# Value loads of batches 3 to 7 spread over their own batch, and q/k loads of batches 4 to 7 moved five steps later, in a fused attention and feed-forward kernel

## The chip, the cores and the metric

One core of one Trainium2 chip. The metric is the device time of one execution in microseconds (us); lower is better. TensorE is called PE, its weight loads PEld, VectorE DVE, ScalarE ACT, GpSimd POOL and SyncE SP; "SPq" is SP's sequencer, which here only issues transfers. Each run lists its mean granted TensorE clock; 1.000 is full speed. A kernel's runs are compared with runs of the kernel before on the same chip.

## The reference

Sliding-window attention with a linear position bias, 8 batches, 8 heads, 576 positions, 64 values a head, then a feed-forward layer on the 4608 rows of 512:

```python
scores = scale * np.matmul(q, k.transpose(0, 1, 3, 2))
mask = (rel >= 0) & (rel < 128)
scores = np.where(mask, scores + bias[None], -1000000000.0)
attn = np.exp(scores - np.max(scores, axis=-1, keepdims=True))
attn = attn / (np.sum(attn, axis=-1, keepdims=True) + 1e-09)
x = (attn @ v).transpose(0, 2, 1, 3).reshape(4608, 512)
h = x @ w_in                                   # 512 -> 2048
out = (h * (1.0 / (1.0 + np.exp(-beta * h)))) @ w_out
```

## The kernel before

A batch has five blocks of rows (128, 128, 128, 128, 64). From batch 3 on, each block of q and k takes this way: SP loads it in float32 (256 KB each), POOL casts it to bfloat16, SP transposes it by DMA into `QK[b % 2]`. Values are loaded and cast in one transfer that POOL issues. The order of all instructions on PE, SP and POOL is fixed by hand: `merge` puts "jobs" at places counted in steps of PE's attention work, and the feed-forward matmuls of earlier batches are spread between the steps.

```python
def load_v(b, sb):
    to = VS[b % 2][0 : ROWS[sb], sb, :, 0:D]
    if b >= NTE:                                    # NTE = 3
        nc.gpsimd.dma_start(out=to, in_=v[b, :, ...].rearrange("h p d -> p h d"))
        return
    ...
def TD(b, sb):                                      # q, then k
    for i in range(2):
        nc.sync.dma_start_transpose(out=QK[b % 2][:, i, :, P * sb : ...], in_=...)
...
for b in range(NTE, B):
    for sb in range(NQB):
        casts = []
        t0 = first[b] - 26 + 4.3 * sb               # first[b]: step of the first scores
        jobs.append((t0, lambda ...: c.append(load_qk(b, sb))))
        jobs.append((t0 + 4.5, lambda c=casts: c.pop()()))
        jobs.append((t0 + 8.5, lambda ...: TD(b, sb)))
        vals(b, sb, first[b] - 7 + 3 * sb)
...
jobs.sort(key=lambda j: j[0])
```

The scores of a batch come in four visits of PE (`SC`, matmuls `sps`). The first two need q of blocks 0 to 2 and k of blocks 0 and 1; the third is the first to need block 4. In the feed-forward part `hps` is the first matmul and `ops` the second.

The softmax here doesn't subtract the row's maximum and nothing guards it: scores larger than these inputs give would overflow.

## Time and profile before

| | |
|---|---|
| time | 332.25 us, median of 3 runs (331.75 to 333.48) |
| PE busy | 318.6 of 329.8 us |
| longest wait of PE | 2.5 us, once, at 95.6 us, for a transpose of batch 3 |
| mean clock of the profiled run | 0.995 |

The prediction below shows the lines of PE, of the wait and of SP's queue. What POOL did meanwhile is in its timeline (start, length, engine, what, idle before):

```profile
81.20 0.89 POOL L137 DMA_DIRECT2D vs<-in_v_dram  x1
...
85.61 0.61 POOL L129 CAST bst<-fst 64x512 bf16<-64x512 f32 x1 [1.37 <-DMA fst<-in_k_dram]
86.17 0.88 POOL L137 DMA_DIRECT2D vs<-in_v_dram  x1
87.04 0.57 POOL L413 DMA_DIRECT2D out_dram<-osb  x1
87.61 0.89 POOL L137 DMA_DIRECT2D vs<-in_v_dram  x1
```

The cast at 85.61 is that of batch 3's last block; its transposes were issued only at 90.24 and after. Between them lie loads of batch 4 on SP, and loads of batch 3's values on POOL.

### The profile page before, as it was taken

How to read it: one execution, taken by the hardware profiler on the slowest of the kernel's cores; microseconds unless marked ns; L12 is line 12 of the kernel's file. 1: busy time of each engine (PE TensorE's matmuls, PEld its weight loads, DVE VectorE, ACT ScalarE, POOL GpSimd, SP SyncE). 2: the span in 40 equal slices, each digit the busy share in tenths (PEclk: the TensorE clock that was granted, in tenths of full speed). 3: DMA queues.
4: the chain of work that ended last, by engine and by line, in shares of the span. 5: the costliest groups of instructions: out<-in, count | busy, mean ns of one | idle time of the engine just before them, and what ended most of it. 6: DMA issues, size and time to landing. Idle time of an engine off the chain costs nothing.

```text
span 329.8 us, 6229 instructions
## 1 busy us (share of the span) xinstructions
PE 318.6 (97%) x2300; PEld 155.8 (47%) x2300; DVE 193.2 (59%) x421; ACT 213.4 (65%) x414; POOL 107.4 (33%) x173
## 2 busy tenths in 40 slices
PE   8999999999969999999999999999999999999995
PEld 3454455445534555454445444544455444444442
DVE  6678679983435776666666766666665543344310
ACT  5657776878756777777777777777774444454421
POOL 4756492244542652614334423530000000000000
PEclk9999999999998999999999999999999999999999
DMA  7999999999999999799999999893121210001111
GB/s 198 252 205 279 192 262 211 220 179 176 167 225 219 197 205 214 108 156 164 185 178 128 152 143 231 122 167 51 40 66 55 79 35 32 34 32 56 41 66 64
DMA packets 136174, 47.67 MB, mean 145 GB/s; under 512 B 123200, under 2 KB 133712, under 8 KB 136144
## 3 DMA queue, kind: packets, MB, share of 16 engines
q1 hardware_dynamic: 105744, 31.60, 51.8%
q0 software_dynamic: 30224, 15.54, 32.8%
q8 instruction: 18, 0.29, 0.4%
q10 hardware_dynamic: 176, 0.14, 0.1%
q14 instruction: 12, 0.10, 0.1%
HBM read 36.71 MB, written 9.44 MB: 140 GB/s over the span
## 4 chain that ended last, share of the span: by engine, by line
PE 85%; DMA 5%; DVE 4%; SPq 3%; ACT 1%; issue 1%; POOL 1%; POOLq 0%
PE hps L379 36%; PE ops L395 33%; PE sps L290 5%; DMA fst<-in_k_dram 4%; PE pv L334 3%; PE pv L330 2%; SPq L253 2%; PE sps L276 2%; PE w L218 1%; PE tps L229 1%; DMA qkT<-bst 1%; DVE qkT L234 1%; DVE gT L385 1%; PE xt L359 1%; SPq L95 1%
## 5 line engine op out<-in xcount | busy, mean ns | idle before, releaser
L384 ACT ACTIVATE sig<-hps,beta_h 128x512 bf16<-128x512 f32 x144 | 99.8, 695 | 78.7 <-PE hps L379 64.0
L379 PE MATMUL hps<-XT,W 128*128 128x512 bf16 x576 | 147.4, 379 | 0.5 <-DVE gT L385 0.4
L395 PE MATMUL ops<-W,gT 128*128 128x512 bf16 x576 | 146.3, 381 | 0.1
L385 DVE SCALAR_TENSOR_TENSOR gT<-sig,hps 128x512 bf16<-128x512 bf16 x144 | 98.3, 684 | 64.2 <-ACT sig L384 63.7
L395 PEld LDWEIGHTS <-gT 128*128 128x128 bf16 x576 | 53.6, 98 | 63.1 <-issue 2.9
L379 PEld LDWEIGHTS <-W 128*128 128x128 bf16 x576 | 51.7, 98 | 52.9 <-issue 3.5
L303 ACT ACTIVATE pt<-sps,bias 128x256 bf16<-128x256 f32 (+1 forms) x192 | 72.9, 493 | 4.1 <-PE sps L290 4.1
L129 POOL CAST bst<-fst 128x512 bf16<-128x512 f32 (+1 forms) x50 | 32.9, 659 | 77.7 <-DMA fst<-in_q_dram 51.2
L307 DVE TENSOR_TENSOR pt<-pt,mask 128x1024 bf16<-128x1024 bf16 x48 | 34.4, 718 | 37.3 <-ACT pt L303 37.1
L413 POOL DMA_DIRECT2D out_dram<-osb x32 | 17.9, 560 | 94.1 <-ACT osb L410 94.1
L340 DVE TENSOR_TENSOR xn<-pv,zs 128x256 bf16<-128x256 f32 (+1 forms) x80 | 33.7, 423 | 2.6
L410 ACT ACTIVATE osb<-ops 128x512 f32<-128x512 f32 x35 | 20.9, 597 | 15.2 <-PE ops L395 15.2
L334 PE MATMUL pv<-vs,pt 128*128 128x65 bf16 x320 | 28.6, 193 | 0.3 <-DVE qkT L234 0.3
L334 PEld LDWEIGHTS <-pt 128*128 128x128 bf16 x320 | 21.6, 97 | 10.3 <-issue 0.6
L290 PE MATMUL sps<-qkT 64*128 64x256 bf16 (+2 forms) x320 | 22.2, 254 | 3.4 <-DMA qkT<-bst 2.5
L330 PE MATMUL pv<-vs,pt 128*128 128x65 bf16 x256 | 24.0, 193 | 0.3 <-DVE XT L365 0.3
L330 PEld LDWEIGHTS <-pt 128*128 128x128 bf16 x256 | 20.1, 98 | 7.3 <-issue 0.7
L290 PEld LDWEIGHTS <-qkT 64*128 64x128 bf16 x320 | 11.4, 95 | 22.1 <-issue 14.8
L298 ACT ACTIVATE pt<-sps 128x1024 bf16<-128x1024 f32 x16 | 16.3, 1023 | 8.2 <-PE sps L290 7.7
L137 POOL DMA_DIRECT2D vs<-in_v_dram x25 | 21.4, 855 | 0.3 <-issue 0.2
L339 DVE RECIPROCAL zs<-pv 128x4 f32<-128x4 f32 (+1 forms) x80 | 13.9, 175 | 9.6 <-PE pv L334 9.4
L113 POOL CAST bst<-fst 128x512 bf16<-128x512 f32 x24 | 14.4, 617 | 13.8 <-DMA fst<-in_q_dram 11.3
(49 smaller groups left out, 113.3 us busy)
## 6 DMA issues: line engine op xcount, KB each, us to landing
fst<-in_q_dram SPq DMA_DIRECT2D x32, 256.0 KB, 4.7
fst<-in_k_dram SPq DMA_DIRECT2D x32, 256.0 KB, 5.1
out_dram<-osb POOLq DMA_DIRECT2D x32, 256.0 KB, 3.5
fst<-in_v_dram SPq DMA_DIRECT2D x12, 256.0 KB, 6.5
vs<-in_v_dram POOLq DMA_DIRECT2D x20, 128.0 KB, 5.1
W<-in_moe_w_in_dram POOLq DMA_DIRECT2D x4, 512.0 KB, 7.2
W<-in_moe_w_out_dram POOLq DMA_DIRECT2D x4, 512.0 KB, 13.7
fst<-in_q_dram SPq DMA_DIRECT2D x8, 128.0 KB, 4.1
```

The source lines that it names most:

```text
L129: nc.gpsimd.tensor_copy(out=t[0 : ROWS[sb], i], in_=f)
L137: nc.gpsimd.dma_start(out=to, in_=v[b, :, P * sb : P * sb + ROWS[sb], :].rearrange("h p d -> p h d"))
L290: nc.tensor.matmul(o, lhsT=qk[64 * e : 64 * e + 64, 1, p, P * kb : P * kb + P], rhs=qk[64 * e : 64 * e + 64, 0, p, P * kb : P * kb + nq], ...
L303: nc.scalar.activation(out=pt[:, e, cols], in_=sps[e][:, cols], func=ACTF.Exp, scale=qscale, bias=bias[:, half, h : h + 1],)
L307: nc.vector.tensor_tensor(out=pt[:], in0=pt[:], in1=masks[m][:].rearrange("p (o c) -> p o c", o=1).broadcast_to([P, 2, 512]), op=ALU.mult,)
L330: nc.tensor.matmul(pv[:, hl, 0 : D + 1], lhsT=weights(b, qb - 1, h, 1), rhs=vs[:, qb - 1, h, 0 : D + 1], start=True, stop=False,)
L334: nc.tensor.matmul(pv[:, hl, 0 : D + 1], lhsT=weights(b, qb, h, 0), rhs=vs[:, qb, h, 0 : D + 1], start=qb == 0, stop=True,)
L340: nc.vector.tensor_tensor(out=xn[0:nq, 4 * g : 4 * g + 4, :], in0=pv[0:nq, :, 0:D], in1=zs[0:nq].broadcast_to([nq, 4, D]), op=ALU.mult,)
L379: nc.tensor.matmul(hps[:], lhsT=W1[:, c, bass.ts(j, P)], rhs=XT[:, c, c0 : c0 + TOKG], start=(c == 0), stop=(c == NDM - 1),)
L384: nc.scalar.activation(out=sig[:], in_=hps[:], func=ACTF.Tanh, scale=beta_h[:, j : j + 1])
L385: nc.vector.scalar_tensor_tensor(out=gts[g][:, j, :], in0=sig[:], scalar=1.0, in1=hps[:], op0=ALU.add, op1=ALU.mult)
L395: nc.tensor.matmul(ops_[:], lhsT=gT[:, j, i * P : i * P + P], rhs=W2[:, j, :], start=(j == 0), stop=(j == NFF - 1),)
```

## The change

The intent: take other transfers out of the way of batch 3's last transposes, and make the rest pay for it as late as they can. In steps, batch 4's first two loads stood at first[3] - 5 and first[3] - 0.7, batch 3's last transposes at first[3] - 0.3; after the change the loads stand at first[3] and later.

```diff
-                t0 = first[b] - 26 + 4.3 * sb
+                t0 = first[b] - (26 if b == NTE else 21) + 4.3 * sb
...
-                vals(b, sb, first[b] - 7 + 3 * sb)
+                vals(b, sb, first[b] + 4.3 * sb - 0.5)
```

## The prediction

> **What bounds the kernel now.** I read the page first (busy shares and slices), then who PE waited for, then the chain of waits around the one long wait, then short windows for the clock, and last the timelines of the two queues that issue transfers. The page says that TensorE is the bound, with one visible dent:
>
> ```profile
> PE 318.6 (97%) x2300; PEld 155.8 (47%) x2300; DVE 193.2 (59%) x421; ACT 213.4 (65%) x414; POOL 107.4 (33%) x173
> ...
> PE   8999999999969999999999999999999999999995
> ...
> PEclk9999999999998999999999999999999999999999
> DMA  7999999999999999799999999893121210001111
> ```
>
> Each slice is 8.2 us. From the second slice on PE is full except in slice 12 (counted from 1), around 91 to 99 us, and the clock digit dips right behind it. DMA digits are at 9 until about 215 us and near 1 after it, so the loads are front-loaded. The longest wait of PE, by who ended it (total, times, longest):
>
> ```profile
> PE sps L290 <- DMA qkT<-bst: 2.5, 1, 2.5
> ```
>
> One wait, once, 2.5 us: a score matmul of batch 3 waits for a DMA transpose of q and k. The next is 1.2 us at the very start, the rest 0.8 us and less. The chain of waits (start, length, what) shows it and what follows:
>
> ```profile
> 93.88 4.19 DMA qkT<-bst
> 98.07 0.05 issue
> 98.12 0.82 PE sps L290 x10
> 98.94 1.82 PE ops L395 x4
> 100.76 1.07 PE hps L379 x4
> ```
>
> and the same kind of visit undisturbed, 34 us later:
>
> ```profile
> 132.77 0.55 PE sps L290 x12
> 133.31 0.97 PE ops L395 x4
> 134.28 0.86 PE hps L379 x4
> ```
>
> The transpose landed at 98.07. The four ops matmuls behind the wait took 1.82 instead of 0.97 us. The windows (PE, PEld, DVE, ACT, POOL busy; then clock, DMA share, GB/s) say why:
>
> ```profile
> 97.00:98.00 1.00, 0.00 (x0) 0.00 (x0) 0.00 (x0) 0.00 (x0) 0.93 (x2) 0.81 1.03 205
> 98.00:99.00 1.00, 0.88 (x11) 0.63 (x12) 0.00 (x0) 0.45 (x2) 0.00 (x0) 0.50 1.41 163
> ```
>
> The granted clock was half from about 97.6 to 101.04 (0.81 is 0.38 us at half, then three windows at 0.50, then 0.98, which is 0.04 us: 3.4 us). Finally the queue that issues q/k loads and transposes (SP, in order):
>
> ```profile
> 80.40 0.66 SPq L95 DMA_DIRECT2D fst<-in_q_dram  x1
> 81.11 0.62 SPq L95 DMA_DIRECT2D fst<-in_k_dram  x1
> 81.78 0.62 SPq L95 DMA_DIRECT2D fst<-in_q_dram  x1
> 82.44 0.61 SPq L95 DMA_DIRECT2D fst<-in_k_dram  x1
> 83.16 5.13 SPq L253 DMA_TRANSPOSE qkT<-bst  x2
> ...
> 90.24 7.50 SPq L253 DMA_TRANSPOSE qkT<-bst  x4
> ```
>
> The loads at 80.40 and 81.11 are batch 3's last rows; 81.78 and 82.44 are already batch 4's. The pair at 83.16 transposes batch 3's fourth block, and the first two of the four at 90.24 its fifth, the one PE waits for. The pair before, at 77.56, took 2.78 us to issue; here it took 5.1, and the first transpose at 90.24 held the queue until about 93.8. Its cast was done at 86.22 (GpSimd timeline: 85.61 plus 0.61), so data was not the reason, the queue was. In the same stretch GpSimd issued value loads of batch 3 at 81.20, 86.17, 87.61 and 90.63, and the DMA share rose to 2.43 in 86:88 and 2.96 in 88:90 (1.26 at 78:80, with 260 GB/s) while 88:90 moved 65 GB/s.
>
> **What the Trainium skill says.** "DMA: Bandwidth & Descriptors", section Anatomy of one DMA: a semaphore wait happens on the issuing sequencer before dispatch, so what stands ahead in SP's queue delays what follows. The order above agrees. Same page, section Issuing engines are not separate DMA queues: transfers started by any engine end on the same 16 DMA engines and interleave. The trace fits (transposes slow where GpSimd's value loads are in flight), though it does not prove it. "TensorE: Matmul & The Clock Gate", section Part 1: The HAM clock gate: after an idle window of about 3.4 us the clock drops to 4/8, and windows are free-running, 3413 ns. The 3.4 us at 0.50 agree; here an idle of only 2.5 us was enough. These waits therefore cost twice: the idle, and the half-speed stretch behind it.
>
> **The change part by part.** No arithmetic is touched. The order of PE, DVE and ACT instructions is the same in both builds except for buffer numbers; SP and GpSimd are reordered.
>
> 1. Batch 4's q/k loads move five steps later, so in SP's order batch 3's fourth and fifth transposes now stand before any load of batch 4. A step: batches 4 and 5 start their scores at 115.93 and 149.18 in PE's timeline, 33.25 us for 23 steps, 1.45 us each; five are 7.2 us. Estimate for the fifth block: its k load was issued at 81.11; with fewer transfers beside it, it lands by about 84.5, the cast ends by 85.1, two transposes (1.2 to 2 us each) are issued by 88, landing by 91. PE wants it just after 95.33, so some 4 us to spare. The wait goes.
>
> 2. Batch 3's value loads no longer come ahead of its first scores (five at first score minus 7 and every 3 steps before; now minus 0.5 and every 4.3). This takes three or four 128 KB loads out of 81 to 92 us. Values are first used long after: at 102.53, 111.43, 113.64, 120.18, 129.53 for the five blocks. In GpSimd's new order they follow the stores and would be issued near 86, 88, 95, 98 and 108; at 5 us to landing each is early by 5 us or more. No new wait of PE on values.
>
> 3. What comes off the path. In the undisturbed visit, ops starts 0.55 us after the first score matmul; so without the wait it would start at 95.33 + 0.55 = 95.88, instead of 98.94: 3.06 us. The half clock then costs (1.82 - 0.97) + (1.07 - 0.86) = 1.06 us. Together 4.1 us. Behind it PE is without gaps to the end (20.00 of 20 us in every 20 us window from 100 to 300), so every microsecond gained there arrives at the end, unless a new gap takes it.
>
> 4. The price: later transposes for batches 4 to 7. Landing of the third block's q transposes against the first score, before: batch 4 110.0 against 115.93, batch 5 133.2 against 149.18, batch 6 170.9 against 181.69, batch 7 207.8 against 214.32. Moved 7.2 us, batches 4 and 7 would be late by 1.3 and 0.7 us if all else kept its time. But it doesn't: batch 4's chain suffered from the same congestion, and batch 7's stood behind X transposes.
>
> **The rivals.** (a) *The wait is gone and nothing replaces it*: 332.25 - 4.1 = 328.1. For: the slack in 1 and 2. (b) *The wait moves to batch 4's first scores*. In the new order, estimated from loads at about 88, casts 1.5 us, pairs of 2.8 us and about 5 us per block, its third block lands near 109 to 110; PE would be there at 115.93 - 4.1 = 111.8. Two microseconds of slack, and a miss costs 1 to 2 us, plus up to 1 us of clock: 329 to 331. (c) *X transposes hold the queue*. In the new order the third block of batches 5, 6 and 7 stands just behind an X transpose that needs the attention output of the batch before (ready at 141.1, 173.7 and 206.2, in times of before). The scores follow 8.0 us later each time. Before, from an X issue to the landing of the next q transpose took 3.6 to 7.2 us. So it mostly fits, but each is a place for a stall of up to 1.5 us: 329 to 331. (d) *The gain is hidden by another engine*. Against: ACT 65% and DVE 59%, and no other wait of PE over 0.5 us after 60 us. (e) *Congestion and not order was the cause, and the value loads only carry it elsewhere*: then new stalls spread over batches 4 to 7, near 332. Against: from 130 us on pairs issue in about 2.5 us with the old value loads beside them.
>
> **Range and chances.** I take 4.1 us off, and give back 0.4 us for (b) and (c) (about one chance in three of a stall of some 1.3 us): 328.5 us. The runs of before spread from 331.75 to 333.48, so the range is 327.2 to 331.0. Faster by over 2% would need under 325.6, more than PE's idle time and cold stretch after start-up hold: 0.02. Slower by over 2%: 0.01. Within 2%: 0.97.
>
> **What would show it.** Right: no wait of PE for the transposes at batch 3, no clock below 1.00 between 90 and 110 us, the SP queue issuing batch 3's last pair before 88, PE busy up from 97% to 98%, and ops at the same place starting about 3 us earlier with 0.97. Wrong: a new wait of PE on these transposes just before the first scores of batch 4, 5, 6 or 7 (near 112, 145, 178, 210 us), a wait of PE on values, or a second half-clock stretch.

## The result, and the profile after

329.75 us, median of 6 runs (328.62 to 330.53), against 333.51 us for the kernel before in 6 runs (331.75 to 335.15). The ratio is 0.9889, 95% interval 0.9851 to 0.9928, an interval that leaves out 1; two runs of the kernel before against itself, below, show how far such an interval can be trusted. (A ratio is the mean time of one kernel's runs over that of the other's runs of the same rounds, so not quite the ratio of the medians. Executions over 1.5% slower than the fastest of the same kernel are left out of the means.) The page of the profile after:

```profile
PE 315.0 (96%) x2258; PEld 155.4 (47%) x2300; DVE 194.4 (59%) x421; ACT 213.6 (65%) x414; POOL 106.8 (33%) x173
...
PE   8889999999999999999999999999999999999995
...
PEclk9999999999999999999999999999999999999999
DMA  7999999999799999989999999999222200001011
```

The 6 in PE's digits and the 8 in the clock's are gone. PE's busy time fell as well, from 318.6 to 315.0 us, though that is not all gain: 42 of its 2300 matmul records are missing here, and a cold matmul counts as longer busy. The prediction's sign "PE busy up from 97% to 98%" did not come: it is 96% here, and 97% in a second profile with all records. DMA is at 9 up to the same place, or one slice later, so nothing was saved there, only moved. PE's waits between 80 and 240 us in the profile after (total, times, longest) begin with:

```profile
PE sps L290 <- DMA qkT<-bst: 0.2, 1, 0.2
```

2.5 us have become 0.2, and the 0.2 is elsewhere: at 113.9 us, the first scores of batch 4. The queue of SP after, at the same place as before:

```profile
81.49 0.66 SPq L95 DMA_DIRECT2D fst<-in_q_dram  x1
82.20 0.62 SPq L95 DMA_DIRECT2D fst<-in_k_dram  x1
82.94 6.04 SPq L253 DMA_TRANSPOSE qkT<-bst  x4
89.03 0.59 SPq L95 DMA_DIRECT2D fst<-in_q_dram  x1
89.67 0.89 SPq L95 DMA_DIRECT2D fst<-in_k_dram  x1
```

All four transposes of batch 3's last two blocks go out right behind their own loads, the last by 88.98, and batch 4's loads follow. And PE at the visit where it had waited:

```profile
96.98 0.61 PE L290 MATMUL sps<-qkT 64*128 64x256 bf16 x12
97.53 1.04 PE L395 MATMUL ops<-W,gT 128*128 128x512 bf16 x4
98.40 1.03 PE L379 MATMUL hps<-XT,W 128*128 128x512 bf16 x4
```

Twelve score matmuls in one go, and `ops` four in 0.87 us from start to next start (1.68 before, 98.87 to 100.55).

Times in the two traces can't be laid side by side, since this run reached batch 3 1.65 us later (its start-up has waits of 1.1 us for weights that the first profile lacks). So measure from batch 3's first score to batch 4's first: 32.20 us before (83.72 to 115.93), 28.25 after (85.37 to 113.62). The difference, 3.95 us, is what the change did in these two profiles. It is more than the spans' difference of 2.0 us, mostly because of the later start.

### The profile page after: what moved, and what is told of

Same layout as the page of the kernel before. It is cut to its first block, busy times and chain, and to the rows that moved or that the text cites. A ratio compares the mean times of both kernels' runs of the same rounds, so it can differ in the third digit from the quotient of the medians.

```text
span 327.8 us, 6185 instructions
## 1 busy us (share of the span) xinstructions
PE 315.0 (96%) x2258; PEld 155.4 (47%) x2300; DVE 194.4 (59%) x421; ACT 213.6 (65%) x414; POOL 106.8 (33%) x173
## 4 chain that ended last, share of the span: by engine, by line
PE 59%; DMA 22%; SPq 8%; POOL 4%; ACT 3%; DVE 2%; issue 2%; POOLq 0%
PE ops L395 29%; PE hps L379 25%; DMA fst<-in_k_dram 11%; DMA fst<-in_v_dram 6%; SPq L253 4%; DMA fst<-in_q_dram 3%; PE sps L290 2%; DMA qkT<-bst 2%; SPq L109 2%; SPq L95 2%; ACT pt L303 2%; PE pv L334 2%; POOL bst L129 1%; PE pv L330 1%; DVE gT L385 1%
## 5 line engine op out<-in xcount | busy, mean ns | idle before, releaser
L379 PE MATMUL hps<-XT,W 128*128 128x512 bf16 x554 | 144.0, 379 | 2.1 <-DMA W<-in_moe_w_in_dram 1.1
L395 PE MATMUL ops<-W,gT 128*128 128x512 bf16 x560 | 143.7, 379 | 1.4 <-issue 0.3
L129 POOL CAST bst<-fst 128x512 bf16<-128x512 f32 (+1 forms) x50 | 31.9, 645 | 78.2 <-DMA fst<-in_q_dram 52.8
L307 DVE TENSOR_TENSOR pt<-pt,mask 128x1024 bf16<-128x1024 bf16 x48 | 35.3, 735 | 34.6 <-ACT pt L303 34.4
L113 POOL CAST bst<-fst 128x512 bf16<-128x512 f32 x24 | 14.3, 619 | 13.5 <-DMA fst<-in_q_dram 8.8
## 6 DMA issues: line engine op xcount, KB each, us to landing
W<-in_moe_w_out_dram POOLq DMA_DIRECT2D x4, 512.0 KB, 13.4
```

The source lines that it names most:

```text
L129: nc.gpsimd.tensor_copy(out=t[0 : ROWS[sb], i], in_=f)
L307: nc.vector.tensor_tensor(out=pt[:], in0=pt[:], in1=masks[m][:].rearrange("p (o c) -> p o c", o=1).broadcast_to([P, 2, 512]), op=ALU.mult,)
L379: nc.tensor.matmul(hps[:], lhsT=W1[:, c, bass.ts(j, P)], rhs=XT[:, c, c0 : c0 + TOKG], start=(c == 0), stop=(c == NDM - 1),)
L395: nc.tensor.matmul(ops_[:], lhsT=gT[:, j, i * P : i * P + P], rhs=W2[:, j, :], start=(j == 0), stop=(j == NFF - 1),)
```

## The experiments

Theory A, mine after the prediction: either part alone is enough, since each takes a delay out. Theory B: the order in SP's queue alone decides. Theory C: the value loads' congestion alone decides. The second question was the size: how much of the gain is the wait, how much the half clock behind it, and is it there in every run? In order of time, the first four runs (values alone, q/k alone, PE kept busy, kernel before again) and the last four (changed kernel again, batch 4 rematch, kernel before a third time, four earlier) were on one chip (called A), the four between on another (B). On each chip the runs of the kernel before, to which ratios refer, are shared.

### The value loads alone

```diff
-                vals(b, sb, first[b] - 7 + 3 * sb)
+                vals(b, sb, first[b] + 4.3 * sb - 0.5)
```

> The value loads spaced as in the changed kernel, q and k of batches 4 to 7 as before, so two loads of batch 4 still stand ahead of batch 3's last transposes. Theory A (either part alone is enough, each takes one of two delays out): no wait of PE at batch 3 over 0.5 us, the pair of transposes for the fifth block issued by 89 us, time ratio to before 0.987 to 0.993. Theory B (only the order in the SP queue counts): a wait of 1.5 us or more stays and a half-clock stretch follows, ratio 0.997 to 1.003. Theory C (only the congestion by value loads counts): as A here.

Measured: 330.85 us, ratio 0.9916 (0.9868 to 0.9963). PE's wait between 80 and 240 us, then SP's queue:

```profile
PE sps L290 <- DMA qkT<-bst: 1.8, 1, 1.8
```

```profile
83.52 0.63 SPq L95 DMA_DIRECT2D fst<-in_q_dram  x1
84.19 0.78 SPq L95 DMA_DIRECT2D fst<-in_k_dram  x1
85.08 5.18 SPq L253 DMA_TRANSPOSE qkT<-bst  x2
90.31 0.59 SPq L95 DMA_DIRECT2D fst<-in_q_dram  x1
90.95 0.57 SPq L95 DMA_DIRECT2D fst<-in_k_dram  x1
91.63 7.26 SPq L253 DMA_TRANSPOSE qkT<-bst  x4
```

No value load is left before or beside the pair of transposes at 85.08, and it still takes 5.18 us to issue (5.13 before). Two of the four value loads are left by the next pair (89.20 and 91.91), and the four transposes take 7.26 us (7.50 before). The wait stays, so theory A falls for batch 3; theory C falls with the next run, which has no wait with all the old value loads in place. Theory B is right about the wait, but its half clock and its ratio (0.997 to 1.003) did not come. The time alone would have misled: the ratio lies in the range of theory A. Why it does comes below, with the clock.

### The q and k loads alone

```diff
-                t0 = first[b] - 26 + 4.3 * sb
+                t0 = first[b] - (26 if b == NTE else 21) + 4.3 * sb
```

> The q and k loads of batches 4 to 7 five steps later, value loads as before, so batch 3's value loads still run into its last transposes. Theory A: no wait of PE at batch 3 over 0.5 us, ratio 0.987 to 0.993; the first transposes of the fourth and fifth block may take 2 to 3 us to issue, but they start about 5 us earlier. Theory B (order): as A. Theory C (congestion by value loads): a wait of 1.5 us or more stays, ratio 0.997 to 1.003.

Measured: 331.17 us, ratio 0.9938 (0.9890 to 0.9986). No wait at batch 3, as B says, but the page is not clean:

```profile
PE sps L290 <- DMA qkT<-bst: 4.9, 3, 2.2
```

Three new waits: 1.86 us at batch 4's first scores, 0.84 at batch 6's, 2.18 at batch 7's. None of my theories had them here. Before batch 7, POOL and SP of this run:

```profile
206.33 1.79 POOL L137 DMA_DIRECT2D vs<-in_v_dram  x2
208.11 0.58 POOL L413 DMA_DIRECT2D out_dram<-osb  x1
```

```profile
208.02 1.21 SPq L355 DMA_TRANSPOSE XT<-xn  x1
209.34 3.61 SPq L253 DMA_TRANSPOSE qkT<-bst  x2
```

and of the changed kernel:

```profile
205.61 0.70 POOL L137 DMA_DIRECT2D vs<-in_v_dram  x1
206.30 0.58 POOL L413 DMA_DIRECT2D out_dram<-osb  x1
```

```profile
206.06 2.06 SPq L355 DMA_TRANSPOSE XT<-xn  x1
208.24 2.51 SPq L253 DMA_TRANSPOSE qkT<-bst  x2
```

With two value loads and a store just ahead, the third block's q transpose took 6.5 us from issue to landing, that is, to the arrival of its data (209.34 to 215.87); with one and a store, 3.6 us (208.24 to 211.84). Five steps later, the third block's transpose falls among the old, bunched value loads, and it has no time to spare. So the two parts aren't two cures for one wait: the later q/k loads cure batch 3, and the spread values pay for the later q/k loads. The 4.9 us are those of this run's slowest execution, the profiled one (333.24 us); by the medians of chip A, bunched values cost some 1.6 us (331.17 against 329.57 of the changed kernel again).

### How much each pair of loads in front costs

Two runs vary the number of batch 4's load pairs ahead of batch 3's last transposes: one (values spread as in the change), and three plus a pair of transposes (values as before).

```diff
# three_later, against the changed kernel
-                t0 = first[b] - (26 if b == NTE else 21) + 4.3 * sb
+                t0 = first[b] - (26 if b == NTE else 23) + 4.3 * sb
# four_earlier, against the kernel before
-                t0 = first[b] - 26 + 4.3 * sb
+                t0 = first[b] - (30 if b == NTE + 1 else 26) + 4.3 * sb
```

> The changed kernel with q and k of batches 4 to 7 three steps later instead of five: one pair of loads of batch 4 stands ahead of batch 3's last pair of transposes, none ahead of the pair before it. If each pair of loads in front costs its own delay (theory of the order): the last transpose lands 1 to 5 us before PE wants it, no wait of PE at batch 3 over 0.5 us, and batches 4 to 7 have 1 to 3 us more to spare than in the changed kernel, so no wait at all there; ratio 0.985 to 0.992. If any load in front is enough to lose: a wait of 1 us or more at batch 3, ratio 0.992 to 0.999.

> The kernel before with batch 4's q and k four steps earlier still: three pairs of loads and one pair of transposes of batch 4 then stand ahead of batch 3's last pair of transposes instead of two pairs of loads. Measured from batch 3's first score, that transpose landed at about 4.3 us with no pair in front, 8.6 with one, 13.4 with two; at some 4.5 us for each pair it lands at 18 to 22 now, and PE wants it at 11.9: a wait of 6 to 10 us, with a half clock of 3.4 us or more in it and behind it. Ratio 1.010 to 1.025. If the wait has nothing to do with what stands in front, it stays at 1.5 to 3 us and the ratio at 1.00.

Measured: one pair 329.54 us, ratio 0.9950 (0.9913 to 0.9986, chip B); three pairs 338.67 us, ratio 1.0155 (1.0085 to 1.0225, chip A). SP's queue with one pair in front (the loads at 85.47 and 86.10):

```profile
82.82 2.59 SPq L253 DMA_TRANSPOSE qkT<-bst  x2
85.47 0.58 SPq L95 DMA_DIRECT2D fst<-in_q_dram  x1
86.10 0.56 SPq L95 DMA_DIRECT2D fst<-in_k_dram  x1
86.78 4.17 SPq L253 DMA_TRANSPOSE qkT<-bst  x2
```

The pair with no load of batch 4 in front goes out in 2.59 us, the one behind two loads in 4.17. Landing of batch 3's last transpose, from batch 3's first score, by the trace; PE wants it at 11.9:

| pairs of loads in front | landed at, us | wait of PE, us |
|---|---|---|
| none (changed kernel, twice) | 6.9, 7.5 | none |
| none, value loads as before (q/k alone) | 7.9 | none |
| one | 9.0 | none |
| two, values spread | 13.6 | 1.8 |
| two (kernel before, three profiles) | 14.3, 13.8, 15.1 | 2.5, 1.9, 3.2 |
| three and a pair of transposes | 17.8 | 5.7 |

Four more profiles with none in front, all with spread values (the two of batch 4 alone, eight later, batch 7's values bunched), gave 6.7 to 8.3 us. So the loads in front decide, with about 1 to 6 us for each pair; the old value loads can't be seen with none in front (7.9), and with two in front the kernel before is 0.1 to 1.4 us later than the run with spread values. The table gives k's transpose, the last; the expectation for three pairs counted from q's, which landed at 4.3 (none), 8.6 (one), 13.4 (two) and here 17.4 us (three). No run issued the same loads at the same time from another queue, so whether it is their place in SP's queue or their traffic that delays the transposes is not told apart; moving them later removes both. The wait with three pairs, 5.7 us, came out just under the 6 to 10 I expected. The one-pair version met its expectation at batch 3, but not at the end, where it had a wait of 0.5 us at batch 7, nor in its ratio (0.985 to 0.992 expected).

### PE kept busy during the wait

```diff
-            SC(b, m, p)
+            SC(b, m, p, fill=12 if (b, m, p) == (NTE, 1, 0) else 0)
```

> The kernel before, with 12 matmuls of zeros (512 columns each, 12 x 0.216 = 2.6 us) ahead of batch 3's first score matmul of its second half, into the same PSUM bank that it then starts afresh: PE stays busy while the transpose lands. The result stays right. If the half clock behind the wait comes from the idle, no record shows a clock under 1.00 near 98 to 101 us, the ops matmuls behind take 0.97 us instead of 1.82, and the time falls by about 1.0 us (ratio 0.995 to 0.999, if the transpose lands when it did). If the clock drops for another reason (load, chance), it stays at half for 3.4 us there and the time is the same or longer.

Measured: 332.38 us, ratio 0.9962 (0.9919 to 1.0005), result correct. PE of this run:

```profile
96.54 2.75 PE L218 MATMUL sps<-zero 128*128 128x512 bf16 x12
99.23 0.61 PE L290 MATMUL sps<-qkT 64*128 64x256 bf16 x12
99.78 1.04 PE L395 MATMUL ops<-W,gT 128*128 128x512 bf16 x4
```

No idle, no half clock, `ops` at full speed. As expected; but a single profile without a half clock proves little, as the next run shows. More telling: none of the six executions had a mean clock of 0.995 or less, against 13 of 24 of the kernel before on this chip (below). And from batch 3's first score to batch 4's it took 30.75 us against 32.20 in the first profile, with the transpose landing nearly as late (14.0 and 14.3 us after the first score). That puts the half clock's own cost at 1.2 to 1.4 us. The interval of the time includes 1, so by time it is open; the median isn't below the 331.41 us of the kernel before's runs at clock 1.000, so no gain beyond the clock is to be seen.

### The kernel before, again

> The kernel before itself, for a second profile: the wait at batch 3 again, 1.5 to 4 us, followed by a half-clock stretch of 3.4 us or a multiple; ratio 0.997 to 1.003. It shows how far the start (the first 60 us) moves from profile to profile: if the changed kernel's later start of about 1.7 us is chance, this one's start differs from the first profile's by something like it.

> The kernel before, a third profile: a wait of 1.5 to 3 us at batch 3. If the rule is that the clock halves when PE idles about 2 us or more inside one window of a fixed 3.41 us grid, this profile shows a half-clock stretch only if one of its windows holds 2.0 us of the idle, and none if the grid splits it below 1.9. Ratio 0.996 to 1.004, which also shows what this comparison can resolve.

Measured: 331.82 us, ratio 0.9954 (0.9893 to 1.0014); and 331.21 us, ratio 0.9937 (0.9890 to 0.9985). The second interval leaves out 1 for the very same code, and both ratios lie outside what I had expected of it (0.997 to 1.003 and 0.996 to 1.004): the comparison resolves no better than some 0.6%, and the half-clock stretch expected of the first did not come. Windows of the second profile (us, busy times, then clock, DMA share, GB/s), and then of the third:

```profile
97.00:98.00 1.00, 0.00 (x0) 0.00 (x0) 0.52 (x1) 0.45 (x1) 1.00 (x2) 1.00 0.98 275
98.00:99.00 1.00, 0.14 (x6) 0.14 (x8) 0.17 (x1) 0.00 (x0) 0.75 (x2) 1.00 0.78 133
99.00:100.00 1.00, 1.00 (x14) 0.53 (x9) 0.00 (x0) 0.81 (x3) 0.00 (x0) 1.00 1.26 115
```

```profile
98.00:99.00 1.00, 0.00 (x0) 0.00 (x0) 0.00 (x0) 0.00 (x0) 0.90 (x2) 1.00 1.33 256
99.00:100.00 1.00, 0.04 (x2) 0.04 (x4) 0.00 (x0) 0.00 (x0) 0.93 (x2) 1.00 0.81 130
100.00:101.00 1.00, 1.00 (x13) 0.59 (x14) 0.00 (x0) 0.71 (x2) 0.00 (x0) 1.00 1.18 100
```

PE idled 1.92 us in the one and 3.23 us in the other, and the clock stayed at 1.00 in both, while 2.50 us in the first profile halved it. So it isn't the length of the idle alone. In every profile the clock record changes on a grid of 3.41 us, and the rule holds: what counts is the idle inside one window of that grid.

| idle of PE | its parts by window, us | clock halved? |
|---|---|---|
| before, 2.50 | 2.02 + 0.49 | yes |
| before again, 1.92 | 0.08 + 1.84 | no |
| before, third, 3.23 | 1.59 + 1.64 | no |
| values alone, 1.78 | 1.78 | no |
| q/k alone, 1.86 / 2.18 | 0.64 + 1.22 / 1.86 + 0.32 | no / no |
| eight later, 1.95 / 3.21 / 2.12 | 0.42 + 1.54 / 3.21 / 2.12 | no / yes / yes |
| four earlier, 5.72 | 1.61 + 3.41 + 0.70 | yes, 6.83 us |

Between 1.86 us (no) and 2.02 us (yes) of 3.41 lies the limit, in all ten idles above. (The end of a run, where PE's work runs out, fits: a window with 1.88 us of idle was not followed by half clock in the changed kernel again, one with 2.11 us was in the rematch. No matmul is left when such a drop comes, so it costs nothing, but it lowers a mean clock to between 0.997 and 0.999.) From batch 3's first score to batch 4's first the three profiles of the kernel before took 32.20, 30.25 and 31.55 us, the changed kernel 28.25 and 28.23. So a wait costs its length and 0.1 us (30.25 - 28.23 = 2.02 for 1.92; 31.55 - 28.23 = 3.32 for 3.23), and the half clock another 1.4 us (32.20 - 28.23 = 3.97 for 2.50).

Every run lists its mean clock, and one half stretch of 3.41 us in 330 lowers it by 0.005. On chip A the 24 runs of the kernel before fall into groups: 9 at 1.000, mean 331.41 us; 10 at 0.995, mean 333.95 us; five others. The groups differ by 2.5 us, more than the 1.4 of the half clock: a longer wait is likelier to lose the clock, and these times don't separate the two. On chip B only 1 of 11 was at 0.995 and 8 were at 1.000 (mean 330.81 us). None of the six runs with the value loads alone was at 0.995: its wait of 1.8 us seems to stay under the limit. That fits its good ratio against a pool in which many runs have the half clock; against the kernel before in its own six runs of that session (331.82) it gained 0.97 us.

### Eight steps instead of five

```diff
-                t0 = first[b] - (26 if b == NTE else 21) + 4.3 * sb
+                t0 = first[b] - (26 if b == NTE else 18) + 4.3 * sb
```

> The changed kernel with q and k of batches 4 to 7 eight steps later. The transposes land three steps (4.4 us) later still: from the changed kernel's 0.2 us of wait at batch 4 and 3.1, 2.5 and 0.5 us to spare at batches 5, 6 and 7, waits of 3 to 5 us at batch 4, 1 to 4 us at 5 and 6 and 3 to 5 us at 7, some with a half-clock stretch of 3.4 us behind. Time 6 to 18 us over the changed kernel, ratio to before 1.01 to 1.04. If instead the queue has slack that the steps don't show, waits stay under 1 us and the ratio is 0.987 to 0.993.

Measured: 341.0 us, ratio 1.0304 (1.0254 to 1.0354, chip B).

```profile
PE sps L290 <- DMA qkT<-bst: 7.3, 3, 3.2
```

Waits of 1.95, 3.21 and 2.12 us at batches 5, 6 and 7, two half-clock stretches, and none at batch 4, where I expected 3 to 5 us. Batch 4's order in the queue is the same as with five steps up to its third block, and no X transpose (attention output of the batch before) stands in that stretch; its loads seem to go at the queue's pace. From batch 5 on, X transposes stand in between, and they wait for the attention of the batch before: SP issued nothing from 127.2 to 137.7 us, up to such a transpose. The changed kernel sits close to this edge: its third block's q made PE wait 0.24 us at batch 4 and landed 3.1, 2.5 and 0.4 us before the first score at 5, 6 and 7 (in its second profile 3.1, 2.6 and 0.0).

### Batch 4 alone, batch 7's values bunched, and the changed kernel again

```diff
# batch4_only and batch4_rematch, against the changed kernel
-                t0 = first[b] - (26 if b == NTE else 21) + 4.3 * sb
+                t0 = first[b] - (21 if b == NTE + 1 else 26) + 4.3 * sb
# bunch7, against the changed kernel
-                vals(b, sb, first[b] + 4.3 * sb - 0.5)
+                vals(b, sb, first[b] - 7 + 3 * sb if b == B - 1 else first[b] + 4.3 * sb - 0.5)
```

> The changed kernel with only batch 4's q and k five steps later, batches 5 to 7 as before. If the gain of the changed kernel is all at batch 3: no wait at batch 3, up to 0.5 us at batch 4, none at 5 to 7 with several us to spare there; ratio 0.985 to 0.992, as the changed kernel. If moving batches 5 to 7 matters: a wait of over 1 us at one of them or at batch 3.

> The changed kernel with the value loads of batch 7 alone back at their old places (first score minus 7, every 3 steps). If value loads close together slow the transposes of the third block beside them: a wait of 1 to 3 us at batch 7's first scores and none new at batches 4 to 6, the transpose taking 5 us or more from issue to landing there (3.6 us in the changed kernel). If the waits in the run with q and k alone had another cause: no wait over 0.5 us at batch 7. Ratio 0.988 to 0.997.

> The changed kernel itself, on the same chip as the next two, for the size of the gain: no wait of PE at batch 3, no half clock after the start. If the gain is the wait of about 2 us always and the half clock of 1 to 1.5 us in some runs only, the ratio to before is 0.990 to 0.995; if the first comparison's 0.9889 holds everywhere, 0.987 to 0.990.

> The version with only batch 4's q and k five steps later and all value loads spaced, again, beside the changed kernel. It has more time to spare at batches 5 to 7, so no wait of PE on transposes over 0.3 us; but the changed kernel loses only some 0.2 to 0.7 us there, so the two should not be told apart: its ratio to before within 0.003 of the changed kernel's.

Measured:

| run | us, median | ratio to before (95%) | chip | waits over 0.3 us at batches 3 to 7 |
|---|---|---|---|---|
| batch 4 alone | 329.32 | 0.9955 (0.9915 to 0.9996) | B | none |
| batch 7's values bunched | 331.40 | 0.9985 (0.9929 to 1.0041) | B | 0.5 at batch 7 |
| changed kernel again | 329.57 | 0.9885 (0.9828 to 0.9941) | A | none for transposes |
| batch 4 alone, rematch | 329.28 | 0.9882 (0.9839 to 0.9925) | A | 0.7 at batch 4 |

The first and the last are one kernel, so the gain it shows is 0.45% on chip B and 1.2% on chip A. Its own time is the same on both, 329.3; what differs is the kernel before, 331.2 on B and 333.8 on A, in step with how many of its runs had the half clock. My expectation of 0.985 to 0.992 on B missed for that reason. The changed kernel again came out in the range set for a gain that is the same everywhere (0.987 to 0.990), but this does not decide the question: 7 of the 12 runs of its pool were at 0.995. Against the kernel before's own six runs of the same session (331.21) it gained 1.6 us. One of its own six executions was slow, 339.08 us at clock 0.990, and is left out of the ratio; no profile of it was kept, so its cause is not known. On chip A batch 4 alone is level with the changed kernel (0.0003 apart), as expected; moving batches 5 to 7 as well makes no difference that can be told apart. The rematch's wait of 0.7 us at batch 4 missed the 0.3 I had set: in the five profiles with the same order up to there, the third block's q of batch 4 landed from 0.1 us before to 0.9 us after the first score. No version tried beats the changed kernel by what can be told apart.

The bunched values came out weaker than expected: batch 7's q transpose did take 6.9 us from issue to landing (204.3 to 211.2; 3.6 in the changed kernel), but PE waited 0.5 us, and the version three steps later had such a wait with spread values. Its ratio, too, missed the 0.988 to 0.997 (one of four executions was slow, 335.96 us, and is left out). Nor is bunching all that slows this transpose: with spread values it took 5.1 and 5.2 us in the two runs of batch 4 alone, and with bunched ones 3.3 to 4.5 in the kernel before, where it falls among other transfers. That bunched values cost PE a wait at batch 7 rests mainly on the run with q and k alone.

## Why the prediction was right

- **The total.** 328.5 predicted, range 327.2 to 331.0; 329.75 measured. The predicted gain was 3.75 us from 332.25, the measured one 3.76 from 333.51. That agreement is partly luck of the chip, as the half clock comes and goes.
- **Part 1, the order.** Right, and shown four ways: with the value loads alone the wait stays, with q and k alone or one pair in front it is gone, with three pairs it is 5.7 us. (The section of the Trainium skill cited for it, Anatomy of one DMA, tells of transfers that GpSimd issues; for SP's queue these runs show it.) I estimated the last pair issued by 88 and landed by 91; it was 88.98 and 92.2 in a run that reached batch 3 1.65 us later.
- **Part 2, the value loads.** "No new wait of PE on values" held. But they were not part of batch 3's cure, which this part and the reading of the congestion ahead of it suggested: the issue took 5.18 us without them. The text also counts "three or four" loads taken out of 81 to 92 us, though by its own new places, near 86 and 88, two of the four stay there; so it was in the profile after (87.27 and 88.71). Their worth is at batches 4, 6 and 7, where leaving them bunched cost 4.9 us of waits in one profile. I listed that congestion as rival (e) only for the case that they carry it elsewhere. The passage of the Trainium skill cited for it, "DMA: Bandwidth & Descriptors", section Issuing engines are not separate DMA queues, says that transfers interleave on the same 16 engines whoever starts them; the 6.5 us against 3.6 at batch 7 fit it, without proving it.
- **Part 3, what comes off.** 3.06 + 1.06 = 4.1 us; the stretch between the two batches' scores shrank by 3.95. But the 1.06 was taken as certain (and came out nearer 1.4). It belongs to the runs in which the grid puts 2 us of idle into one window: at least 10 of 24 on one chip, 1 of 11 on the other, by their mean clocks. Without it the gain is about 2 us (331.41 at clock 1.000 to 329.57 again, on chip A).
- **Part 4 and rivals (b), (c).** Two microseconds of slack were estimated at batch 4; PE waited 0.24 us there in one profile and under 0.1 in the next. At batches 5 to 7, 8 us between X and score against 4 to 7 needed leaves 1 to 4; it was 3.1, 2.5 and 0.4. No stall of 1.3 us came, so the 0.4 us given back were not needed, but the edge is real: three steps more cost about 11 us (341.0 against some 329.5). There batch 4 had no wait: my counting in steps did not hold for it.

## What to carry to other kernels

In a queue that issues in order, look at what stands ahead of the transfer that PE will want next: two pairs of loads for a later batch cost this one 1.8 to 3.2 us of PE, and moving them behind it was the cure. When transfers are moved later, their neighbours must be moved too, or the wait comes back at the next batch; test each part of such a change alone and read the waits, not the time. And when runs of one kernel spread by a per cent, sort them by granted clock before averaging: a ratio then shows how often the baseline fell into the slow clock as much as what the change did.

## What the Trainium skill lacked or had wrong

- "TensorE: Matmul & The Clock Gate", section Part 1: The HAM clock gate, and its advice there against idle gaps over about 3.4 us: it speaks of one idle window of that length. Here 2.02 us of idle within one 3.41 us window halved the clock, 1.86 us did not, and 3.23 us of idle split 1.59 + 1.64 over two windows did not. The free-running grid and the length of the stretch (3.41 us, or two of them) agree with the page.
- "DMA: Bandwidth & Descriptors": we found no figure there for how long a DMA transpose holds the issuing queue when loads are in flight ahead of it. Here a transpose alone was issued in about 1.2 us, and the first one behind batch 4's 256 KB loads took 3.8 and 3.5 us (83.16 to 86.99, with four of SP's loads in flight, and 90.24 to 93.78, with two); in the other profiles with this order it was 3.0 to 4.0. The cause inside the queue is not shown by any run.
- None has this: in three profiles of one kernel, the one before, PE reached batch 3's first score at 83.72, 84.85 and 85.05 us, so 1.3 us of the spread lie before the change begins to matter.
